# Four float32 head pairs of a windowed attention: values held stationary and weights scaled before the transposes

## The chip, the cores and the metric

One core of one Trainium2 chip runs the program. The metric is the device time in microseconds. Engines are named as the profile names them: PE (TensorE, with PEld for its weight loads), DVE (VectorE), ACT (ScalarE), POOL (GpSimd) and SP (SyncE, which issues the transfers here).

## The reference

The input is q, k and v of 4 batches, 8 heads, 768 positions and 64 values a head, in float32. Each query attends to the 128 positions up to its own (`window`) and to the first 4 positions (`n_sink`). A gated feed-forward layer follows, from 512 to 2048 and back, over 3072 tokens.

```python
scores = scale * np.matmul(q, k.transpose(0, 1, 3, 2))
scores = np.where(keep, scores, -1000000000.0)
scores = scores - np.max(scores, axis=-1, keepdims=True)
a = np.exp(scores)
a = a / (np.sum(a, axis=-1, keepdims=True) + 1e-09)
attn = np.matmul(a, v)
...
h = x @ w_in
g = h * np.clip(h + 3.0, 0.0, 6.0) / 6.0
out = g @ w_out
```

## The kernel before

The work is cut into units of 256 positions (3 a batch, 12 in all) and, in each unit, into 4 pairs of heads: 48 pieces, numbered `s`. The 128 partitions of a piece hold two heads of 64 values each. The first 16 pieces are the first units of the 4 batches. They see only their own 256 positions, so two tiles of 128 queries against 128 and 256 keys, and they run in plain float32: `plain(s)` is true. All other products (the feed-forward layers and the later pieces) run as sums of rounded float32 parts.

The steps of a plain piece, each with the letter that it has in the written order:

- `S.s.t` (`S_plain`, L374): scores of tile t, both heads, each head on its own 64 rows of the array, PE.
- `M.s.h.t` (`S_least`, L387): mask and the least value, DVE. Two records each, the second reads the accumulator.
- `X.s.h.t` (`X_exp`, L422): the exponential in place in `Ph`, ACT.
- `T.s.h` (`T_plain`, L481): three 128x128 transposes of `Ph`, PE.
- `C.s.h` (`T_copy`, in the helper `copy_r`, L37 on ACT or L43 on DVE): the transposed weights to `pf`. There is one buffer `pf`, so `C` of a piece waits for the last product that reads `pf` of the piece before.
- `E.s.h` (`E_plain`, L530): three products with 65 columns, the stationary side is `pf`. The 65th column of the values is ones, so it gives the row's sum.
- `R.s`, `U.s`, `V.s` (L429, L430, L435, L444): sum plus 1e-9, reciprocal, rows scaled on DVE; then two transposes on PE.
- `x.s`, `y.s` (`x_high`, `x_low`, L37 or L43, L588): the result is cut into a rounded part and a rest.

`w.j.1` to `w.j.6` (`W_decode`) make a block of weights out of 64-bit words: two passes on ACT (L193, L198), two on DVE (L201, L204), a rounding copy and a difference (L209). They take 0.7 to 1.7 us each. `F`, `G` and `O` are pieces of the first feed-forward units.

For this first part of the program the string `FIRST` is the order. It is written out by hand, and every engine runs its own instructions in that order; nothing overtakes. So `T.4.1` is not only a place on PE: whatever `T_plain` issues on ACT or DVE stands there in the queues of ACT and DVE too. Around the change it reads:

```
X.4.0.1 V.1 S.5.1 C.3.0 l.9 X.4.0.0 X.4.1.1 C.3.1 S.5.0 T.4.0 X.4.1.0 R.2 W.3 x.1 E.3.0 U.2
w.0.1 W.4 y.1 T.4.1 M.5.1.0 E.3.1 ... V.2 M.5.0.0 S.6.1 R.3 C.4.1 x.2 C.4.0 T.5.1 U.3 X.5.0.0 S.6.0
... E.4.1 w.0.3 x.3 X.6.0.0 T.5.0 X.6.0.1 S.7.0 C.5.0 S.7.1 R.4 y.3 C.5.1 T.6.0 U.4 w.2.2 E.5.0 w.0.4 V.4 E.5.1
... T.6.1 y.4 S.9.1 ... x.5 S.9.0 X.8.1.0 E.6.1 l.10 y.5 X.7.0.1 M.8.0.1 w.2.1 T.7.1 M.8.1.1 T.7.0 R.6 C.7.1 F.0.0.0
```

The scores, the transposes, the products and the sums in PSUM share one ring of 8 banks.

Of the kernel before, what the change touches and what calls it, by code (L numbers as in the profile page):

```python
# [9 lines left out]
F32 = mybir.dt.float32  # L10
# [36 lines left out]
def attn_ffn_kernel(ctx: ExitStack, tc: tile.TileContext, qx, kx, vx, px, vsx, limits, w_in, w_out, out):  # L47
    nc = tc.nc
# [3 lines left out]
    H, D, UT = 2 * NP, 64, 256  # L52
# [7 lines left out]
    ps = fast.enter_context(tc.tile_pool(name="ps", bufs=8, space=PSUM))  # L60
# [22 lines left out]
    tiny = const.tile([P, 1], F32, name="tiny")  # L83
    nc.vector.memset(tiny, 1e-9)

    def keep_busy(n, src):

        idle = ps.tile([P, 512], F32, tag="bank", name="idle")
        for _ in range(n):
# [183 lines left out]
    def plain(s):  # L273
        return s < NF32 and pus[s][1] == 0
# [76 lines left out]
    def cell(s, h, t, c0, c1):  # L351

        if plain(s):
            return st_[s]["P"][:, h, t * P + c0:t * P + c1]
        return st_[s]["P"][:, h, t * WP + c0:t * WP + c1]
# [54 lines left out]
    def norm(e, blk, c):  # L410
        if e == "A":
            nc.scalar.mul(out=blk, in_=blk, mul=c)  # L412
        elif e == "D":
            nc.vector.tensor_scalar(out=blk, in0=blk, scalar1=c, scalar2=None, op0=ALU.mult)
        else:
            nc.gpsimd.tensor_scalar(out=blk, in0=blk, scalar1=c, scalar2=1.0, op0=ALU.mult, op1=ALU.mult)

    def X_exp(s, h, t):
        d, i = st_[s], 2 * h + t
        blk = cell(s, h, t, 0, spans(pus[s][1])[t][1])  # L420
        if plain(s):
            nc.scalar.activation(out=blk, in_=blk, func=AF.Exp, scale=-1.0, bias=d["nb"][:, i:i + 1])  # L422
            return
        nc.scalar.activation(out=blk, in_=blk, func=AF.Exp, scale=-1.0,  # L424
                             bias=d["nb"][:, i:i + 1], accum_out=d["sm"][:, i:i + 1])

    def R_plain(s):
        d = st_[s]
        nc.vector.tensor_scalar(out=d["sm"], in0=d["av"][:, :, D], scalar1=1e-9, scalar2=None, op0=ALU.add)  # L429
        nc.vector.reciprocal(out=d["rc"], in_=d["sm"])  # L430

    def U_plain(s):
        d = st_[s]
        d["rows"] = work.tile([P, 2, 2, D], F32, tag="tmp", name="rows", bufs=1)
        nc.vector.tensor_tensor(out=d["rows"].rearrange("p t h d -> p h t d"),  # L435
                                in0=d["av"][:, :, 0:D].rearrange("p (h t) d -> p h t d", h=2),
                                in1=d["rc"].rearrange("p (h t) -> p h t", h=2).unsqueeze(3).to_broadcast([P, 2, 2, D]),
                                op=ALU.mult)

    def V_plain(s):  # L440
        d = st_[s]
        d["xp"] = ps.tile([P, UT], F32, tag="bank", name="xp")
        for t in range(2):
            nc.tensor.transpose(out=d["xp"][:, t * P:(t + 1) * P],  # L444
                                in_=d["rows"][:, t].rearrange("p h d -> p (h d)"), identity=ident)
# [6 lines left out]
    def C_soft(s, h):  # L452
        b, u, p = pus[s]
        d = st_[s]
        rc = d["rc"]
        for t in range(2):
            X_exp(s, h, t)
        if plain(s):
            return
        R_sums(s, h)  # L460
        live = [(P, W2), (P, W2)] if u else [(0, P), (0, 2 * P)]
        if u:

            both = d["P"][:, h].rearrange("p (t w) -> p t w", t=2)[:, :, P:2 * P]
            prior = d["P"][:, h, 0:2 * WP].rearrange("p (t w) -> p t w", t=2)[:, :, 0:P]
            nc.gpsimd.tensor_tensor(out=both, in0=both, in1=prior, op=ALU.add)  # L466
        for t in range(2):
            i, blk = 2 * h + t, cell(s, h, t, *live[t])
            norm(NORM[i], blk, rc[:, i:i + 1])
        if u and h == 1:  # L470

            ss = ssc.rearrange("p (t k h y) -> p t k h y", t=2, k=2, h=2)
            snk_in = d["P"][:, :, 2 * P:2 * WP].rearrange(
                "p h (t y) -> p t h y", t=2)[:, :, :, 0:SK]
            split_parts(nc, ss[:, :, 0], ss[:, :, 1], snk_in, weng(SSE, 0), weng(SSE, 1))

    def T_plain(s, h):
        d = st_[s]
        d["pt", h] = ps.tile([P, 512], F32, tag="bank", name="pt")
        for j, (t, c) in enumerate(((0, 0), (1, 0), (1, P))):  # L480
            nc.tensor.transpose(out=d["pt", h][:, j * P:(j + 1) * P], in_=cell(s, h, t, c, c + P), identity=ident)  # L481
# [7 lines left out]
    def D_pt(s, h):  # L489
        b, u, p = pus[s]  # L490
        d = st_[s]
        if plain(s):
            T_plain(s, h)
            T_copy(s, h)
            return
        pt = ps.tile([P, 512], F32, tag="bank", name="pt")
        for t, c in ((0, P), (1, P + SK)):
            nc.tensor.transpose(out=pt[:, t * P:(t + 1) * P], in_=cell(s, h, t, c, c + P), identity=ident)  # L498
        both = d[f"pt{h}"] = work.tile([P, 8 * P], F32R, tag=f"ph{h}", name="ph", bufs=1)

        def two(a, b, c):
            return both[:, a:b].rearrange("p (t z) -> p t z", t=2)[:, :, c:c + P]

        own, prior = (two(0, 8 * P, 2 * P), two(2 * P, 8 * P, 2 * P)), (two(0, 6 * P, 0), two(0, 8 * P, P))
        split_parts(nc, own[0], own[1], pt[:, 0:2 * P].rearrange("p (t q) -> p t q", t=2), nc.scalar, nc.vector)
        for i in range(2):
            nc.gpsimd.affine_select(out=prior[i], in_=own[i], pattern=[[0, 2], [-1, P]], base=0,  # L507
                                    channel_multiplier=1, compare_op=ALU.is_gt, fill=0.0)
            nc.gpsimd.affine_select(out=own[i], in_=own[i], pattern=[[0, 2], [1, P]], base=0,  # L509
                                    channel_multiplier=-1, compare_op=ALU.is_ge, fill=0.0)  # L510

    def D_snk(s):
# [6 lines left out]
        for t in range(2):  # L519
            rows = slice(4 * SK * t, 4 * SK * (t + 1))  # L520
            nc.scalar.copy(out=pz[rows, t * P:(t + 1) * P], in_=sp[rows, 0:P])  # L521

    def E_plain(s, h):
        d = st_[s]
        if h == 0:
            d["av"] = ps.tile([P, 4, D1], F32, tag="bank", name="av")
        for t in range(2):
            for slot in range(t + 1):
                c = (t + slot) * P
                nc.tensor.matmul(out=d["av"][:, 2 * h + t, :], lhsT=d["pf"][:, h, c:c + P], rhs=d["VS"][:, slot, h, :],  # L530
                                 start=(slot == 0), stop=(slot == t))

    def E_av(s, h):
        b, u, p = pus[s]
        d = st_[s]
        if plain(s):
            E_plain(s, h)
            if h == 1:
                R_plain(s)
                U_plain(s)  # L540
                V_plain(s)
                x_high(s, d["xp"])
            return
# [507 lines left out]
```

## Time and profile before

| | |
|---|---|
| median of 2 runs | 648.54 us (647.94 to 649.13) |
| the profiled execution | 650.11 us, of which the trace spans 648.4 us |
| PE busy | 639.7 us (99%) |
| PEld busy | 573.3 us (88%) |
| DVE busy | 488.1 us (75%) |
| ACT busy | 418.2 us (64%) |
| POOL busy | 180.0 us (28%) |
| the chain of work that ended last | PE 95%, DMA 2%, ACT 1% |

Shares are means over 648 us. The stretch that the change touches is from 17 to about 44 us. PE's durations are longer than the distance from one matmul to the next, since matmuls overlap; where a cost of PE is wanted, the distance between the starts of two groups is the number to take.

### The profile page before, as it was taken

The page shows a single profiled execution, that of the slowest core. Times are in us where ns is not written, and L with a number is a line of the kernel's source. Part 1 is how long each engine was busy: PE and PEld are TensorE (multiplying, and loading weights), DVE is VectorE, ACT ScalarE, POOL GpSimd, SP SyncE. Part 2 cuts the span into 40 slices and gives each one's busy share as a digit, 9 for nine tenths or more (in the row PEclk, how much of TensorE's full clock was granted, in tenths as well). Part 3 has the DMA queues.
Part 4 walks back from the last instruction along what each step waited for, and adds up shares of the span by engine and source line. Part 5 has one row for each costly group of instructions (what it writes and reads, how often), then busy time and mean ns, then how long its engine had stood idle before and what let it go on. Part 6 is the DMA issues. An engine that isn't in the chain of part 4 may idle for free.

```text
span 648.4 us, 11429 instructions
## 1 busy us (share of the span) xinstructions
PE 639.7 (99%) x3492; PEld 573.3 (88%) x3492; DVE 488.1 (75%) x1286; ACT 418.2 (64%) x1048; POOL 180.0 (28%) x337
## 2 busy tenths in 40 slices
PE   9999999999999999999999999999999999999996
PEld 8899878898998998999898989899889998888885
DVE  5998989988777797978788878788788787533331
ACT  5998578768676688667767776678867765311111
POOL 1000000004433544444344434443354344000000
PEclk9999999999999999999999999999999999999999
DMA  6875660057555548544554655445644440100001
GB/s 245 328 249 178 250 218 1 17 153 202 145 132 142 129 122 225 127 112 120 146 131 133 173 135 134 121 113 138 195 127 108 118 108 2 66 0 1 1 0 69
DMA packets 45746, 82.90 MB, mean 128 GB/s; under 512 B 7024, under 2 KB 30832, under 8 KB 43632
## 3 DMA queue, kind: packets, MB, share of 16 engines
q1 hardware_dynamic: 45680, 82.11, 44.1%
q8 instruction: 30, 0.49, 0.3%
q14 instruction: 36, 0.29, 0.1%
HBM read 41.19 MB, written 6.29 MB: 73 GB/s over the span
## 4 chain that ended last, share of the span: by engine, by line
PE 95%; DMA 2%; ACT 1%; SPq 1%; issue 0%; DVE 0%; POOL 0%; ACTq 0%; POOLq 0%
PE hps L675 36%; PE o L685 35%; PE av L551 5%; PE sp L405 4%; PE av L530 3%; PE sp L374 2%; PE pt L498 2%; PE hps L601 2%; PE pt L481 2%; PE o L635 2%; DMA lent<-in_w_in_dram 1%; PE idle L90 1%; DMA K<-kt 1%; PE xp L444 1%; ACT lent L198 0%
## 5 line engine op out<-in xcount | busy, mean ns | idle before, releaser
L675 PE MATMUL hps<-x,w 128*128 128x512 f32 x1104 | 264.5, 384 | 0.0
L685 PE MATMUL o<-w,gh 128*128 128x512 f32 x736 | 223.1, 385 | 0.0
L675 PEld LDWEIGHTS hps<-x,w 128*128 128x128 f32 x1104 | 201.3, 190 | 24.2 <-DVE nb L387 0.2
L685 PEld LDWEIGHTS o<-w,gh 128*128 128x128 f32 x736 | 136.8, 197 | 10.8 <-issue 0.3
L685 PE MATMUL o<-w,g 128*128 128x512 f32 x368 | 139.7, 380 | 0.0
L466 POOL TENSOR_TENSOR Pt<-Pt 128x256 f32<-128x256 f32 x64 | 54.2, 846 | 271.4 <-ACT Pt L424 271.4
L612 ACT ACTIVATE ost<-hps,three 128x512 f32<-128x512 f32 x80 | 54.9, 687 | 86.1 <-PE hps L675 85.3
L617 DVE SCALAR_TENSOR_TENSOR ost<-ost,hps 128x512 f32<-128x512 f32 x80 | 54.8, 685 | 56.4 <-ACT ost L612 55.7
L507 POOL TENSOR_SCALAR_AFFINE_SELECT ph<-ph 128x256 fp32r<-128x256 f32 x128 | 66.7, 521 | 56.8 <-ACT ph L37 56.8
L685 PEld LDWEIGHTS o<-w,g 128*128 128x128 f32 x368 | 72.4, 197 | 7.1
L424 ACT ACTIVATE Pt<-Pt,nb 128x272 f32<-128x272 f32 x128 | 65.7, 514 | 12.2 <-DVE nb L387 12.1
L387 DVE CUSTOM_DVE_ANT_0 Pt<-sp,m_t 128x272 f32<-128x272 f32 x128 | 53.0, 434 | 25.4 <-PE sp L405 19.8
L509 POOL TENSOR_SCALAR_AFFINE_SELECT ph<-ph 128x256 fp32r<-128x256 f32 x128 | 60.3, 471 | 35.7 <-DVE ph L32 30.6
L626 DVE TENSOR_TENSOR g<-ost,gh 128x512 fp32r<-128x512 f32 x80 | 66.3, 829 | 2.4
L412 ACT ACTIVATE Pt<-Pt,rc 128x144 f32<-128x144 f32 x128 | 45.9, 406 | 7.7 <-POOL Pt L466 5.3
L551 PEld LDWEIGHTS av<-ph,VS 128*128 128x128 f32 x192 | 36.2, 189 | 5.2 <-issue 0.6
L405 PE MATMUL sp<-K 128*128 128x272 f32 x256 | 40.6, 280 | 0.0
L37 ACT ACTIVATE ph<-pt 128x256 fp32r<-128x256 f32 x64 | 24.5, 383 | 23.5 <-PE pt L498 22.8
L551 PE MATMUL av<-ph,VS 128*128 128x256 f32 (+1 forms) x192 | 38.5, 310 | 0.2 <-DVE nb L387 0.2
L405 PEld LDWEIGHTS sp<-K 128*128 128x128 f32 x256 | 37.0, 190 | 1.9 <-ACT pz L521 0.2
L43 DVE CAST gh<-ost 128x512 fp32r<-128x512 f32 x80 | 35.6, 445 | 2.4
L554 DVE TENSOR_TENSOR xf<-av,xf 64x256 f32<-64x256 f32 x64 | 26.6, 416 | 7.6 <-ACT xf L553 6.3
(106 smaller groups left out, 839.3 us busy)
## 6 DMA issues: line engine op xcount, KB each, us to landing
K<-kt SPq DMA_DIRECT2D x128, 200.0 KB, 3.4
K<-kt SPq DMA_DIRECT2D x128, 64.0 KB, 2.5
kr<-in_kx_dram SPq DMA_DIRECT2D x32, 200.0 KB, 2.4
vr<-in_vx_dram SPq DMA_DIRECT2D x32, 192.0 KB, 2.5
out_dram<-ost SPq DMA_DIRECT2D x22, 256.0 KB, 2.4
lent<-in_w_in_dram SPq DMA_DIRECT2D x5, 1024.0 KB, 7.6
qr<-in_qx_dram SPq DMA_DIRECT2D x40, 128.0 KB, 2.3
lent<-in_w_out_dram SPq DMA_DIRECT2D x5, 1024.0 KB, 6.4
```

The lines of the kernel that those rows point to most:

```text
L387: nc.vector.tensor_tensor_reduce(out=cell(s, h, t, 0, w), in0=sp[:, 0:w], in1=m[:, 0:w], scale=-SCALE, scalar=3.0e38, op0=ALU.add, op1=ALU ...
L405: nc.tensor.matmul(out=sp[:, 0:w], lhsT=Q[:, h, t * P:(t + 1) * P], rhs=keys, start=(r == 0), stop=(r == 1))
L424: nc.scalar.activation(out=blk, in_=blk, func=AF.Exp, scale=-1.0, bias=d["nb"][:, i:i + 1], accum_out=d["sm"][:, i:i + 1])
L466: nc.gpsimd.tensor_tensor(out=both, in0=both, in1=prior, op=ALU.add)
L507: nc.gpsimd.affine_select(out=prior[i], in_=own[i], pattern=[[0, 2], [-1, P]], base=0, channel_multiplier=1, compare_op=ALU.is_gt, fill=0.0)
L509: nc.gpsimd.affine_select(out=own[i], in_=own[i], pattern=[[0, 2], [1, P]], base=0, channel_multiplier=-1, compare_op=ALU.is_ge, fill=0.0)
L551: nc.tensor.matmul(out=o, lhsT=l, rhs=r, start=(j == 0), stop=(j == len(seq) - 1))
L612: nc.scalar.activation(out=gf, in_=hp, func=AF.Relu, bias=three, scale=1.0)
L617: nc.vector.scalar_tensor_tensor(out=gf, in0=gf, scalar=6.0, in1=hp, op0=ALU.min, op1=ALU.mult)
L626: nc.vector.tensor_tensor(out=g, in0=gf, in1=gh.bitcast(F32), op=ALU.subtract)
L675: nc.tensor.matmul(out=state["h", j], lhsT=l(j // 2)[:, c, fs], rhs=r, start=(c == 0 and k == 0), stop=(c == NP - 1 and k == 2))
L685: nc.tensor.matmul(out=acc, lhsT=l[:, tt * P:(tt + 1) * P], rhs=r(j // 2)[:, j % 2, :].rearrange("p (s d) -> p d s", s=2), start=(j == 0 a ...
```

## The change

Pieces 4 to 7 (the table `NORMED`) leave the plain way. Their exponentials also add up the row (`accum_out`, L424). `T_plain` first makes sum plus 1e-9 (on ACT for head 0, on DVE for head 1), the reciprocal on DVE, and scales both tiles of the weights in place, by the letters of the table: A is ACT (`norm`, L412), D is DVE (L414), in the order head 0 tile 0, head 0 tile 1, head 1 tile 0, head 1 tile 1. Only then come the transposes. `E.s.0` does nothing; `E.s.1` holds 64 columns of values stationary and streams `pf`, 256 queries against the first 128 keys and 128 against the second. Head 0 goes to partitions 0 to 63 and head 1 to 64 to 127 of one bank, `xp`, which is what the two transposes of `V` made before. `R`, `U` and `V` of these pieces do nothing.

```diff
-        if plain(s):
+        if plain(s) and s not in NORMED:
             nc.scalar.activation(out=blk, in_=blk, func=AF.Exp, scale=-1.0, bias=d["nb"][:, i:i + 1])
             return
         nc.scalar.activation(out=blk, in_=blk, func=AF.Exp, scale=-1.0,
...
     def T_plain(s, h):
         d = st_[s]
+        if s in NORMED:
+            sm, rc = (d[x][:, 2 * h:2 * h + 2] for x in ("sm", "rc"))
+            if h == 0:
+                nc.scalar.activation(out=sm, in_=sm, func=AF.Identity, bias=tiny, scale=1.0)
+            else:
+                nc.vector.tensor_scalar(out=sm, in0=sm, scalar1=1e-9, scalar2=None, op0=ALU.add)
+            nc.vector.reciprocal(out=rc, in_=sm)
+            for t in range(2):
+                i = 2 * h + t
+                norm(NORMED[s][i], cell(s, h, t, 0, P * (t + 1)), d["rc"][:, i:i + 1])
         d["pt", h] = ps.tile([P, 512], F32, tag="bank", name="pt")
...
+    NORMED = {4: "AAAA", 5: "DDDD", 6: "AADD", 7: "DDAA"}
+
     def E_plain(s, h):
         d = st_[s]
+        if s in NORMED:
+            if h == 0:
+                return
+            d["xp"] = ps.tile([P, UT], F32, tag="bank", name="xp")
+            for slot, c0, q0 in ((0, 0, 0), (1, UT, P)):
+                for h in range(2):
+                    nc.tensor.matmul(out=d["xp"][D * h:D * (h + 1), q0:UT], lhsT=d["VS"][:, slot, h, 0:D],
+                                     rhs=d["pf"][:, h, c0:c0 + UT - q0], start=(slot == 0), stop=(slot == 1))
+            return
```

The same test with a bare `return` stands at the head of `R_plain`, `U_plain` and `V_plain`. The string `FIRST` is unchanged.

ACT's queue at piece 4, before. The four L422 are its exponentials, x is `x.1`, L193 is `w.0.1`, and the last two rows belong to piece 5:

```order
L422 ACTIVATE Ph<-Ph,nb 128x256
L422 ACTIVATE Ph<-Ph,nb 128x128
L422 ACTIVATE Ph<-Ph,nb 128x256
L422 ACTIVATE Ph<-Ph,nb 128x128
L37 ACTIVATE x_347<-xp 128x256
L193 ACTIVATE wt<-st 128x1024
L422 ACTIVATE Ph<-Ph,nb 128x128
L422 ACTIVATE Ph<-Ph,nb 128x256
```

And the same place of ACT now:

```order
L424 ACTIVATE Ph,sm<-Ph,nb 128x256
L424 ACTIVATE Ph,sm<-Ph,nb 128x128
L424 ACTIVATE Ph,sm<-Ph,nb 128x256
L488 ACTIVATE sm<-sm,tiny 128x2
L412 ACTIVATE Ph<-Ph,rc 128x128
L412 ACTIVATE Ph<-Ph,rc 128x256
L424 ACTIVATE Ph,sm<-Ph,nb 128x128
L37 ACTIVATE x_351<-xp 128x256
L193 ACTIVATE wt<-st 128x1024
L412 ACTIVATE Ph<-Ph,rc 128x128
L412 ACTIVATE Ph<-Ph,rc 128x256
```

The scaling of head 0 stands ahead of the fourth exponential, that of head 1 behind `w.0.1`.

DVE's queue at piece 5, now. L387 are the mask steps of piece 6, L201 is `w.0.3`, L491 and L414 belong to `T.5.0`, and the last row is the reciprocal of `T.6.0`. Before, L201 was followed by `R.4` (L429, L430), and `T.5.0` had nothing on DVE:

```order
L387 ISA Ph,nb<-sp,m_100 128x128
L387 ISA nb 128x1
L201 SCALAR_TENSOR_TENSOR lent<-wt,lent 128x1024
L491 RECIPROCAL rc<-sm 128x2
L414 TENSOR_SCALAR Ph<-Ph,rc 128x128
L414 TENSOR_SCALAR Ph<-Ph,rc 128x256
L615 TENSOR_TENSOR x_435<-xp,x_435 128x256
L491 RECIPROCAL rc<-sm 128x2
```

The reciprocal and the scaling, on which PE's transposes now depend, stand behind the long `w.0.3`.

ACT's queue at piece 7, before. L193 is `w.2.1`, L198 is `w.4.2`, and the L422 are exponentials of pieces 8 and 9:

```order
L193 ACTIVATE wt<-lent 128x1024
L422 ACTIVATE Ph<-Ph,nb 128x256 x2
L198 ACTIVATE lent<-lent 128x1024
L422 ACTIVATE Ph<-Ph,nb 128x128
L422 ACTIVATE Ph<-Ph,nb 128x256 x2
```

And now; L412 is the scaling of `T.7.1`, L488 the sum of `T.7.0`:

```order
L193 ACTIVATE wt<-lent 128x1024
L412 ACTIVATE Ph<-Ph,rc 128x128
L412 ACTIVATE Ph<-Ph,rc 128x256
L488 ACTIVATE sm<-sm,tiny 128x2
L422 ACTIVATE Ph<-Ph,nb 128x256 x2
L198 ACTIVATE lent<-lent 128x1024
```

The scaling for `T.7.1` stands behind `w.2.1`, and the sum of `T.7.0` behind the scaling.

## Rows read from the trace of the kernel before

**Rows 1.** Busy time by stretch: PE, PEld, DVE, ACT, POOL, granted clock, DMA share, GB/s.

```profile
17.30:32.60 15.30, 15.30 (x130) 12.81 (x129) 14.24 (x62) 14.20 (x33) 0.00 (x0) 1.00 0.85 338
```

**Rows 2.** The chain that ended last, 74 to 96 us: start, us, what.

```profile
79.22 0.47 PE sp L374 x4
...
80.56 7.57 DMA lent<-in_w_in_dram
```

**Rows 3.** Timeline of PE, 0 to 70 us: start, us, what.

```profile
18.23 0.93 PE L374 MATMUL sp<-lent 64*128 64x256 f32 x8
19.08 0.55 PE L481 MATMUL pt<-ident_r,Ph 128*128 128x128 f32 x3
19.46 0.78 PE L530 MATMUL av<-lent,pf 128*128 128x65 f32 x6
...
20.50 0.78 PE L530 MATMUL av<-lent,pf 128*128 128x65 f32 x6
21.12 0.39 PE L444 MATMUL xp<-ident_r,rows 128*128 128x128 f32 x2
21.43 0.70 PE L374 MATMUL sp<-lent 64*128 64x256 f32 x4
...
22.55 0.49 PE L374 MATMUL sp<-lent 64*128 64x128 f32 x4
...
24.95 0.93 PE L374 MATMUL sp<-lent 64*128 64x128 f32 x8
...
28.08 1.40 PE L374 MATMUL sp<-kr,qr 64*128 64x256 f32 x8
...
32.60 1.58 PE L601 MATMUL hps<-x,w 128*128 128x256 f32 x12
```

**Rows 4.** Timeline of ACT, 15.8 to 33.5 us.

```profile
17.30 1.49 ACT L422 ACTIVATE Ph<-Ph,nb 128x256 f32<-128x256 f32 x4 [0.28 <-DVE nb L387]
18.70 0.36 ACT L37 ACTIVATE x<-xp 128x256 fp32r<-128x256 f32 x1
18.96 1.14 ACT L193 ACTIVATE wt<-st 128x1024 f32<-128x1024 f32 x1
...
25.12 0.87 ACT L37 ACTIVATE pf<-pt 128x384 f32<-128x384 f32 x2
25.88 1.17 ACT L198 ACTIVATE lent<-lent 128x1024 int32<-128x1024 uint32 x1
...
32.57 0.91 ACT L422 ACTIVATE Ph<-Ph,nb 128x256 f32<-128x256 f32 x2
```

**Rows 5.** Timeline of ACT, 142.7 to 145.2 us, a later piece that sums its rows.

```profile
143.23 0.19 ACT L424 ACTIVATION_READ_ACCUMULATOR Pt<-Pt,nb 128x1 f32 x1
143.32 0.51 ACT L424 ACTIVATE Pt<-Pt,nb 128x272 f32<-128x272 f32 x1
```

**Rows 6.** Instructions of single lines: ns least/median/most, first and last start.

```profile
L412 ACT ACTIVATE Pt<-Pt,rc x128: 397/403/418, 145.1 to 544.0; 128x144 f32<-128x144 f32 x128
L449 ACT ACTIVATE sm<-sm,tiny x64: 280/295/301, 144.3 to 542.9; 128x2 f32<-128x2 f32 x64
L450 DVE RECIPROCAL rc<-sm x64: 147/166/169, 144.8 to 543.2; 128x2 f32<-128x2 f32 x64
L43 DVE CAST x<-xf x9: 275/287/295, 135.8 to 552.8; 128x256 fp32r<-128x256 f32 x9
```

**Rows 7.** Timeline of DVE, 18 to 33.5 us.

```profile
18.16 1.02 DVE L43 COPY pf<-pt 128x384 f32<-128x384 f32 x2 [0.48 <-ACT Ph L422]
...
21.64 0.40 DVE L43 CAST x<-xp 128x256 fp32r<-128x256 f32 x1
...
23.88 1.22 DVE L201 SCALAR_TENSOR_TENSOR lent<-wt,lent 128x1024 int32<-128x1024 int32 x1
```

**Rows 8.** Busy time by stretch after the last matmul; columns as in the first group.

```profile
643.00:645.00 2.00, 0.00 (x0) 0.00 (x0) 0.00 (x0) 0.44 (x1) 0.00 (x0) 1.00 0.57 211
645.00:646.00 1.00, 0.00 (x0) 0.00 (x0) 0.00 (x0) 0.00 (x0) 0.00 (x0) 0.62 0.39 137
```

More of the change, by code (lines that the diff above doesn't have):

```diff
@@ L441, in V_plain @@
         d = st_[s]
+        if s in NORMED:
+            return
         d["xp"] = ps.tile([P, UT], F32, tag="bank", name="xp")
@@ L478, in T_plain @@
         d = st_[s]
+        if s in NORMED:
+            sm, rc = (d[x][:, 2 * h:2 * h + 2] for x in ("sm", "rc"))
[7 more added lines that the diff above has]
+                norm(NORMED[s][i], cell(s, h, t, 0, P * (t + 1)), d["rc"][:, i:i + 1])
         d["pt", h] = ps.tile([P, 512], F32, tag="bank", name="pt")
@@ L521, in D_snk @@
             nc.scalar.copy(out=pz[rows, t * P:(t + 1) * P], in_=sp[rows, 0:P])
+    NORMED = {4: "AAAA", 5: "DDDD", 6: "AADD", 7: "DDAA"}
     def E_plain(s, h):
         d = st_[s]
+        if s in NORMED:
+            if h == 0:
+                return
+            d["xp"] = ps.tile([P, UT], F32, tag="bank", name="xp")
[3 more added lines that the diff above has]
+                                     rhs=d["pf"][:, h, c0:c0 + UT - q0], start=(slot == 0), stop=(slot == 1))
+            return
         if h == 0:
```

## The prediction

> **What bounds the kernel now.** I read the busy time by stretch first, since the means over the whole span say little about a change that ends at 44 us. From 17.3 to 32.6 us PE is busy throughout, and ACT (14.20 of 15.30 us) and DVE (14.24) have about 1 us free each [rows 1]. So three engines are full at once, each in a written order: work taken from PE is worth its time only if ACT and DVE keep up, and work given to ACT or DVE has almost no idle time to go into. Next, the chain that ended last, for what becomes of a delay. It is PE's own work, one piece after another, until a load of weights that begins at 80.56 us; SP could issue it only after PE's scores at 79.22 us had freed a buffer [rows 2], and from that load the chain goes on to later transposes of PE. The load is tied to PE's progress. A lag that PE has collected by 40 us is therefore carried to the end, and so is a lead. Last, the timelines of the three engines between 17 and 33 us, for the walk below.
>
> **PE's own work.** Of each of the four pieces go two `E` and one `V`. An `E` takes 0.62 us (20.50 to 21.12), the three transposes from 19.08 to 19.46 show at most 0.13 us for one, and `V` with the change to the scores takes 0.31 (21.12 to 21.43) [rows 3]. So two transposes are 0.22 and about 0.09 is what entering the scores' form costs; 2 x 0.62 + 0.22 = 1.46 us go. The new product has no row: two 64-column halves, each with 256 and 128 columns streamed. The nearest row is a block of scores, two 64-row halves with 256 and 128 columns, both heads at once: 18.23 to 19.08, 0.85 us [rows 3]; with the 0.09 it is 0.94. If the halves of columns did not run side by side it would be at most twice that, 1.7. I take 0.94, as the shape is the nearest. Gain 0.5 us a piece, 2.1 us in four; bounds 2.1 gained and 1.0 lost.
>
> That halves of the array run side by side the rows show for 64 rows only. The Trainium skill (TensorEngine Tiling, section Tiling Modes) says it of column tiles too; no run here shows it yet. By that the product is 0.94, without it up to 1.7, and as three of the four products stand ahead of a wait that the walk finds, the sum would move by less than 1 us.
>
> **ACT and DVE.** Each exponential now reads its accumulator, 0.09 us (143.23 to 143.32) [rows 5], 16 times: 1.5. Four sums on ACT, 0.295 or less each, as neighbours overlap [rows 6]: about 1. Eight scalings on ACT: one of 144 columns takes 0.40 and the next follows after 0.3 [rows 6], so 0.30 for 128 and 0.40 for 256 columns, as the exponentials do (four in 1.40, 17.30 to 18.70) [rows 4]: 2.8. Together 5.3 us on an engine with 1 us free in the stretch. DVE loses `R` and `U` and gets reciprocals (0.17) and eight scalings; the nearest row for 256 columns out of SBUF is a cast, 0.29, with 0.2 for 128 [rows 6], the bound above is 0.34 (copies of 384 columns out of PSUM, 0.51 each) [rows 7]. That is about even. What counts is where these stand: between exponentials and transposes, behind what was queued earlier. So I walk along the queues.
>
> **The walk.** Times are those of the new run, before in brackets.
>
> 1. `T.4.0`. Three exponentials from 17.30 with three reads end at 17.30 + 1.11 + 0.28 = 18.69. The sum ends at 18.98; the reciprocal stands on DVE behind the two copies that began at 18.16 [rows 7], so 19.10 to 19.27; the scalings end at 19.72 and 20.12. While ACT waits for the reciprocal, its fourth exponential, `x.1` and `w.0.1` are held behind it. The transposes of the second tile start at 20.15, and `E.3.0` at 20.40 [19.46, rows 3]. Lag 0.9.
> 2. `T.4.1`. Behind these on ACT: the fourth exponential (to 20.41), `x.1` (0.26, to 20.67) and `w.0.1` (L193, 1.05 to the next start, to 21.72) [rows 4]. The scalings end at 22.12 and 22.52; `E.3.1` starts at 22.80 [20.50]. Lag 2.3. This wait is new: `w.0.1` was nobody's predecessor on PE.
> 3. `T.5.1`, on DVE. `R.3` waits for `E.3.1`, 22.80 + 0.78 = 23.58; then two small ones and the cast of `x.2` (0.33) [rows 7], 24.28; sum and reciprocal, 24.65; scalings end at 24.85 and 25.10. `S.6.0` at 25.43 [22.55]. Lag 2.9.
> 4. `T.5.0`, on DVE behind `w.0.3`. From the cast to `w.0.3` DVE took 21.64 to 23.88 [rows 7]; without the cast 1.8 to 1.9, so `w.0.3` starts at about 26.8 and ends the queue's hold 1.14 later, 27.95. The ACT sum is ready then too. Reciprocal and scalings end at 28.42 and 28.65, while PE, which finished `V.3` and the new product at 27.0, has idled since. `S.7.0` at 29.0 [24.95]. Lag 4.0.
> 5. `T.6.0` and `T.6.1`. PE ends `T.5.0` at 29.06; ACT copies both `pf` (0.76; 0.87 with the end) [rows 4], sums, waits for DVE's reciprocal at 30.37 and scales until 31.23; the product of piece 5 runs 31.57 to 32.43; `T.6.1`'s scalings on DVE (behind `w.0.4`) end just then, 32.67. `S.9.1` at 33.0 [28.08]. Lag 4.9: the product's saving is in it.
> 6. `T.7.1` and `T.7.0`. ACT leaves the scalings of piece 6 at 31.13 and has the same queue ahead as before from 25.88 to 32.57, 6.69 us [rows 4], with four reads more and 0.2 to 0.3 of idle time less: 37.9. Then come the scalings of `T.7.1` (end 38.28 and 38.68), the sum (38.87), DVE's reciprocal and scalings for `T.7.0` (39.53). On PE the scores of pieces 8 and 9 wait until the copies of piece 6 free their banks (34.4), then comes the product of piece 6, to 35.8; there PE waits 2.5 us for the scalings. `F.0.0.0` at 39.8 [32.60, rows 3]. Lag 7.1.
> 7. After that no scaling is left. The last of the savings (the two `V` and the rest of piece 7's product, 0.5) still come: lag 6.6.
>
> Nothing downstream takes it back: SP's loads shift with PE, and the queues of ACT and DVE are late by about as much (ACT by 6.6). The sum against the profiled run: 650.11 + 6.6 = 656.7, a span of 655.0. That run was 1.6 above the median, so 648.54 + 6.6 = **655.1 us**, 1% slower. 2% (13 us) is about what a measurement of this kernel can tell from no change.
>
> **Rivals.** (a) Clock. By the walk PE idles 1.4 us before `T.5.0` and 2.5 before `T.7.1`. After the last matmul the granted clock was 1.00 up to 645 us and 0.62 in the next one, with no matmul since 643 [rows 8]; so it falls from 2.4 to 1.2 GHz when PE does nothing. If it falls at about 39 us, `F.0.0.0` and what follows run at half speed until it rises; how long that takes no row shows, and if 2 to 4 us of work run at half clock, they add as much: 657 to 659. Against it: the two waits lie 7 us apart, with products and scores between. The Trainium skill (TensorE: Matmul & The Clock Gate, Part 1) says that the gate opens only after sustained activity and closes after idling; by that this rival holds, and the row agrees that it closes. (b) The waits are shorter than walked, since part of ACT's queue was waiting for PE or DVE and closes up: half the lag, 650 to 652. For it: ACT shows idle time ahead of 17.30 and some later [rows 4]. (c) Faster: PE's saving is all that reaches the end, 648.5 - 2.1 = 646.4. The mechanism is that the scalings are done before PE gets to the transposes; it decides when ACT's and DVE's queues run 2.5 us ahead of PE at `T.4.1` and `T.7.1`. Against it, before the change ACT's exponentials end less than 1 us ahead of PE's use at `T.4.0` (four from 17.30 last until 18.79, transposes at 19.08) [rows 3, 4]. (d) Slower still: with the columns' halves one after the other and the later loads of weights colliding, 660 to 664.
>
> **Chances.** The forecast (653 to 657) 0.52, the clock 0.18, half the lag 0.14, faster 0.08, slower still 0.08. The range takes the first three: 650 to 660; outside are faster and slower still, 0.16. Beyond 2% lies only the upper half of the last, 0.05, and on the fast side almost nothing, 0.01.
>
> **What the new profile would show.** `E.3.1` at about 22.8, `F.0.0.0` near 39.8; idle time of PE ahead of L497 put down to ACT L412 and DVE L414, some 6 us in sum; the new product in 0.85 us with both halves starting together; granted clock 1.00 (a), or a stretch at 0.5. I am wrong if the waits of PE ahead of L497 sum to under 3 us, or if PE idles again between 40 and 100 us.

## The result and the profile after

| | before | after |
|---|---|---|
| median of 2 runs | 648.54 us | 658.14 us (658.02 to 658.26) |
| the profiled execution, its span | 650.11, 648.4 us | 658.26, 656.6 us |
| mean granted clock | 0.998 | 0.991 |

The ratio is 1.0144, with a 95% interval of 1.0124 to 1.0164: 1.4% slower, 9.6 us by the medians and 8.2 by the two profiled executions. The interval lies above 1.00 as a whole, so the loss is clear of the scatter although it is under the 2% that the prediction took for the least that can be told. The forecast was 655.1 and the range 650 to 660.

First the busy time by stretch, the view of [rows 1]: PE, PEld, DVE, ACT, POOL, then the granted clock, the share of the DMA engines and GB/s.

```profile
17.30:32.60 15.30, 10.70 (x74) 6.92 (x75) 11.41 (x51) 12.74 (x43) 0.00 (x0) 0.92 0.82 331
32.60:40.00 7.40, 5.69 (x36) 3.79 (x33) 4.16 (x18) 6.33 (x18) 0.00 (x0) 0.70 0.23 63
40.00:50.00 10.00, 9.73 (x71) 8.70 (x72) 7.76 (x22) 7.75 (x16) 0.00 (x0) 0.83 0.54 218
```

PE was full from 17.3 to 32.6 us [rows 1] and is now idle for 4.6 us of it, and for 1.7 of the next 7.4. But all three engines got emptier: ACT fell from 14.20 to 12.74 and DVE from 14.24 to 11.41, though over the whole program ACT is busy for 5.1 us more and DVE for 1.9. Less of the program falls into the stretch, since the engines wait for each other. And the clock column is new: below 1.00 in all three stretches.

The timeline of PE, the view of [rows 3], shows where the idle time stands. In brackets is the idle time ahead of the line, and who ended it. Line numbers shift with each edit: the transposes `T` are L481 before, L497 here, and L487 or L501 in kernels below.

```profile
18.00 0.92 PE L374 MATMUL sp<-lent 64*128 64x256 f32 x8
19.52 0.84 PE L497 MATMUL pt<-ident_r,Ph 128*128 128x128 f32 x3 [0.60 <-ACT Ph L412]
20.19 0.78 PE L557 MATMUL av<-lent,pf 128*128 128x65 f32 x6
21.88 0.84 PE L497 MATMUL pt<-ident_r,Ph 128*128 128x128 f32 x3 [0.90 <-ACT Ph L412]
22.55 0.78 PE L557 MATMUL av<-lent,pf 128*128 128x65 f32 x6
...
25.34 0.49 PE L374 MATMUL sp<-lent 64*128 64x128 f32 x4
...
28.51 0.61 PE L497 MATMUL pt<-ident_r,Ph 128*128 128x128 f32 x3 [1.51 <-DVE Ph L414]
29.05 0.93 PE L374 MATMUL sp<-lent 64*128 64x128 f32 x8
30.89 1.09 PE L497 MATMUL pt<-ident_r,Ph 128*128 128x128 f32 x3 [0.92 <-ACT Ph L412]
31.91 1.55 PE L549 MATMUL xp<-pf,lent 128*64 128x256 f32 x8
...
34.23 2.93 PE L374 MATMUL sp<-kr,qr 64*128 64x256 f32 x16
...
39.59 0.84 PE L497 MATMUL pt<-ident_r,Ph 128*128 128x128 f32 x3 [1.64 <-ACT Ph L412]
...
41.31 2.83 PE L628 MATMUL hps<-x,w 128*128 128x256 f32 x12
...
44.39 0.87 PE L549 MATMUL xp<-pf,lent 128*64 128x256 f32 x8
45.19 0.87 PE L497 MATMUL pt<-ident_r,Ph 128*128 128x128 f32 x6
```

Every wait is ahead of L497, the transposes, and is ended by a scaling (L412 on ACT, L414 on DVE). The new product L549 lasts 0.87 us where the clock is full and 1.55 where it is not; at full clock the next group starts 0.80 us after it (44.39 to 45.19). `F.0.0.0` (L628) lasted 1.58 before [rows 3] and lasts 2.83 here.

The waits of PE from 17 to 60 us, grouped, and after them the longest group of DVE's: us in sum, times, longest.

```profile
PE pt L497 <- ACT Ph L412: 4.1, 4, 1.6
PE pt L497 <- DVE Ph L414: 2.3, 3, 1.5
```

```profile
DVE rc L491 <- ACT sm L488: 2.6, 2, 1.3
```

The same windows as above, one microsecond each, at the edges of the two stretches of half clock:

```profile
30.00:31.00 1.00, 0.10 (x1) 0.11 (x1) 0.76 (x2) 0.77 (x4) 0.00 (x0) 0.64 0.00 0
31.00:32.00 1.00, 1.00 (x5) 0.45 (x7) 1.00 (x6) 1.00 (x2) 0.00 (x0) 0.50 0.00 0
...
37.00:38.00 1.00, 0.96 (x10) 0.49 (x8) 1.00 (x3) 1.00 (x5) 0.00 (x0) 0.95 0.15 22
...
40.00:41.00 1.00, 0.73 (x4) 0.41 (x4) 0.81 (x4) 1.00 (x4) 0.00 (x0) 0.76 1.03 434
...
43.00:44.00 1.00, 1.00 (x7) 1.00 (x7) 1.00 (x5) 0.80 (x3) 0.00 (x0) 0.54 1.00 426
```

The clock falls from 2.4 to 1.2 GHz at about 30.3 us, behind the wait of 1.51 us and 0.3 us into the one of 0.92, and stays there until about 37; it falls again at about 40.5, behind the wait of 1.64, until about 44.

### The profile page after: what moved, and what is told of

Its sections match the earlier page's. It is cut to its first block, busy times and chain, and to the rows that moved or that the text cites. A ratio compares the mean times of both kernels' runs of the same rounds, so it can differ in the third digit from the quotient of the medians.

```text
span 656.6 us, 11414 instructions
## 1 busy us (share of the span) xinstructions
PE 642.1 (98%) x3468; PEld 571.2 (87%) x3468; DVE 490.0 (75%) x1294; ACT 423.2 (64%) x1076; POOL 180.2 (27%) x337
## 4 chain that ended last, share of the span: by engine, by line
PE 91%; ACT 3%; DVE 3%; DMA 1%; issue 1%; SPq 0%; POOL 0%; DVEq 0%; POOLq 0%; ACTq 0%
PE hps L702 35%; PE o L712 35%; PE av L578 5%; PE sp L405 4%; PE pt L514 2%; PE av L557 2%; PE sp L374 2%; PE pt L497 2%; PE o L662 2%; DMA qr<-in_qx_dram 1%; PE hps L628 1%; PE idle L90 1%; ACT Ph L412 0%; PE xp L549 0%; DMA vr<-in_vx_dram 0%
## 5 line engine op out<-in xcount | busy, mean ns | idle before, releaser
L712 PEld LDWEIGHTS o<-w,gh 128*128 128x128 f32 x736 | 136.5, 196 | 11.1 <-issue 0.3
L424 ACT ACTIVATE Pt<-Pt,nb 128x272 f32<-128x272 f32 x128 | 65.7, 514 | 12.7 <-DVE nb L387 12.6
L387 DVE CUSTOM_DVE_ANT_0 Pt<-sp,m_t 128x272 f32<-128x272 f32 x128 | 53.1, 433 | 25.1 <-PE sp L405 21.2
L412 ACT ACTIVATE Pt<-Pt,rc 128x144 f32<-128x144 f32 x128 | 45.9, 406 | 8.0 <-POOL Pt L472 5.1
L37 ACT ACTIVATE ph<-pt 128x256 fp32r<-128x256 f32 x64 | 24.6, 384 | 22.3 <-PE pt L514 21.4
```

Of the source, the lines that this page charges most:

```text
L387: nc.vector.tensor_tensor_reduce(out=cell(s, h, t, 0, w), in0=sp[:, 0:w], in1=m[:, 0:w], scale=-SCALE, scalar=3.0e38, op0=ALU.add, op1=ALU ...
L712: nc.tensor.matmul(out=acc, lhsT=l[:, tt * P:(tt + 1) * P], rhs=r(j // 2)[:, j % 2, :].rearrange("p (s d) -> p d s", s=2), start=(j == 0 a ...
```

## The experiments

Each kernel was timed against the kernel before on the same chip; that one's medians were 647.98 (first four rows), 647.72 (next three), 648.69 (next two) and 648.49 (last two).

| run | median us | ratio | 95% interval |
|---|---|---|---|
| product_alone | 647.05 | 0.9983 | 0.9969 to 0.9996 |
| scaling_alone | 661.32 | 1.0211 | 1.0194 to 1.0228 |
| waits_filled | 655.40 | 1.0116 | 1.0099 to 1.0133 |
| scale_pool | 658.57 | 1.0168 | 1.0148 to 1.0188 |
| changed | 658.79 | 1.0176 | 1.0145 to 1.0207 |
| decode_behind | 657.44 | 1.0147 | 1.0124 to 1.0170 |
| scale_early | 653.30 | 1.0081 | 1.0057 to 1.0105 |
| early_filled | 652.78 | 1.0068 | 1.0046 to 1.0090 |
| early_moved | 655.47 | 1.0105 | 1.0087 to 1.0124 |
| early_scores_first | 652.25 | 1.0049 | 1.0035 to 1.0062 |
| only_45 | 656.74 | 1.0119 | 1.0098 to 1.0139 |

**The two halves of the change apart.** First the product without the scaling (`product_alone`):

```diff
-        if plain(s) and s not in NORMED:
+        if plain(s):
...
     def T_plain(s, h):
         d = st_[s]
-        if s in NORMED:
-            sm, rc = (d[x][:, 2 * h:2 * h + 2] for x in ("sm", "rc"))
...
-                norm(NORMED[s][i], cell(s, h, t, 0, P * (t + 1)), d["rc"][:, i:i + 1])
```

> The new product without the scaling: pieces 4 to 7 keep the stationary values and leave out the row sums, the reciprocals and the scalings, so their results stay unnormalized. Theory (the loss is waiting for the scalings, PE itself gains): no idle time of PE ahead of the transposes of pieces 4 to 7, clock 1.00, PE does 4 x (1.46 - 0.80) = 2.6 us less, and the lead is carried to the end: about 646, ratio to the kernel before 0.996. Rival 1 (the product itself costs, its halves of columns serial or its entry dear): 649 or more. Rival 2 (a lead of PE is not carried, the engines beside it or the loads set the end): 648 to 649.

It is faster than before, by 0.3 to 2.0 us. PE's timeline shows the gain of PE itself, and that it doesn't get all of it:

```profile
17.75 0.92 PE L374 MATMUL sp<-lent 64*128 64x256 f32 x8
...
30.26 0.89 PE L487 MATMUL pt<-ident_r,Ph 128*128 128x128 f32 x6 [0.65 <-DVE x L605]
30.94 1.60 PE L618 MATMUL hps<-x,w 128*128 128x256 f32 x12
```

`F.0.0.0` starts at 30.94 instead of 32.60 [rows 3], 1.7 us earlier. But this execution was early by 0.5 us before the change begins: the scores ahead of `T.4.0`, which the change does not touch, start at 17.75 instead of 18.23 [rows 3]. So the lead is 1.2 us, what three products and two `V` save (1.8) less the wait of 0.65 for DVE. With the savings that follow, PE is some 2 us ahead; the times show 0.9 by the medians, so the truth is between the theory and rival 2.

Then the scaling without the product (`scaling_alone`): `E`, `R`, `U` and `V` of the four pieces as before, on weights that are already normalized.

```diff
     def E_plain(s, h):
         d = st_[s]
-        if s in NORMED:
-            if h == 0:
-                return
...
```

> The scaling ahead of the transposes without the new product: the four pieces are normalized first and then still go through the old product with its column of ones (sums of 1), the scaling of rows and the two transposes. Theory (waits for the scalings): the same waits ahead of the transposes as with both edits, less what the longer product fills of them; 658 to 661, ratio 1.015 to 1.019. Rival (the new product is what costs): 648 to 651.

2.1% slower than before, just above the top of the expected times and ratios. So the way to scaled weights (the summing exponentials, sums, reciprocals and scalings, and the waits for them) is the loss, more than all of it, and the product gives a part back.

**The clock.** `waits_filled` puts spare work where PE would wait:

```diff
+    FILL = {(4, 0): 4, (4, 1): 7, (5, 1): 3, (5, 0): 12, (6, 0): 7, (7, 1): 16, (7, 0): 2}
...
         d["pt", h] = ps.tile([P, 512], F32, tag="bank", name="pt")
+        for _ in range(FILL.get((s, h), 0)):
+            nc.tensor.transpose(out=d["pt", h][:, 0:P], in_=ident, identity=ident)
```

> The changed kernel with spare transposes of the identity put ahead of the transposes that wait (4, 7, 3, 12, 7, 16 and 2 of them for T.4.0, T.4.1, T.5.1, T.5.0, T.6.0, T.7.1 and T.7.0), into the bank that is overwritten next, so that PE works while it would wait. Theory (part of the loss is the clock, which falls because PE idles): clock 1.00 throughout, and the time falls though PE does more: by 1.6 to 4 us, to 654 to 656.5. Rival (the clock is a bystander, its slow stretch hidden behind the waits for ACT and DVE): 657.5 to 658.5, with the clock at 1.00. Third: the spare work does not hold the clock, time 658 to 660.

51 transposes more, and 2.7 us less than the changed kernel (658.14), 3.4 less than its second measurement (658.79, below). These were taken at different times; as losses against the kernel before beside each, 7.4 us stand against 9.6 and 11.1, so 2.2 to 3.7 us are gone. Busy time by stretch of `waits_filled`:

```profile
17.30:32.60 15.30, 14.86 (x112) 10.50 (x112) 11.42 (x53) 12.54 (x41) 0.00 (x0) 1.00 0.84 335
32.60:40.00 7.40, 6.50 (x55) 4.85 (x51) 5.32 (x24) 7.40 (x23) 0.00 (x0) 1.00 0.48 149
40.00:50.00 10.00, 10.00 (x90) 9.19 (x89) 9.25 (x25) 9.29 (x17) 0.00 (x0) 1.00 0.44 167
```

The clock is 1.00 in all three, and DVE and ACT did no more in the first stretch than in the changed kernel (11.42 and 12.54): the spare work took away no wait for them, it only held the clock. The first theory holds. PE's timeline of `waits_filled`, for the walk below:

```profile
18.43 0.92 PE L374 MATMUL sp<-lent 64*128 64x256 f32 x8
...
33.70 1.80 PE L374 MATMUL sp<-kr,qr 64*128 64x256 f32 x16
...
40.29 1.58 PE L632 MATMUL hps<-x,w 128*128 128x256 f32 x12
```

The changed kernel was measured a second time beside the next runs:

> The changed kernel once more, beside these runs: 658, ratio 1.014 to 1.016, clock at half speed in two stretches.

658.79 us; the profiled execution has a mean clock of 0.987. The two stretches that were expected are one here. The clock fell at about 22.3 us, behind waits of 0.60 and 0.91, and stayed down until about 36:

```profile
22.00:23.00 1.00, 1.00 (x9) 1.00 (x8) 0.00 (x0) 0.54 (x3) 0.00 (x0) 0.65 0.89 347
```

That is 13.7 us at half speed where the first trace has some 10 in two stretches, yet the span is the same (656.7 and 656.6), since PE waits less, 4.5 us for the scalings instead of 6.4: half-speed work fills a part of the waits. When the clock falls is not the same in every execution; that it fell is, by the mean clock of all six of this kernel (0.984 to 0.991).

**What the scalings wait for.** `scale_pool` moves them to the engine that has nothing to do:

```diff
-    NORMED = {4: "AAAA", 5: "DDDD", 6: "AADD", 7: "DDAA"}
+    NORMED = {4: "PPPP", 5: "PPPP", 6: "PPPP", 7: "PPPP"}
```

> All 16 scalings on POOL, which has no work from 10 to 150 us, instead of ACT and DVE; sums and reciprocals stay. Theory (the scalings wait behind the decoding of weights in ACT's and DVE's queues): the waits of T.4.1 and T.7.1 shrink by 0.3 to 0.9 each, that of T.5.0 stays, since its sum comes out of ACT's queue at the same time as the decoding ends on DVE; ACT is relieved of 2.8 us: 655 to 657. Rival (POOL is slow or disturbs DVE): each scaling takes over 0.8 us, time 659 or more.

No gain that can be told: 658.57. PE waits 6.4 us for the scalings on POOL, as long as before on ACT and DVE:

```profile
PE pt L497 <- POOL Ph L416: 6.4, 5, 1.9
```

The price of one on POOL is in its timeline (two scalings a line):

```profile
27.29 0.83 POOL L416 TENSOR_SCALAR Ph<-Ph,rc 128x128 f32<-128x128 f32 x2 [3.15 <-DVE rc L491]
30.10 1.62 POOL L416 TENSOR_SCALAR Ph<-Ph,rc 128x128 f32<-128x128 f32 x2 [1.97 <-DVE rc L491]
```

0.83 us for two is no dearer than on ACT (0.80 for two, L412). Taking 2.8 us of scaling off ACT did not help: what comes ahead of a scaling, the sum and the reciprocal, still stands in ACT's and DVE's queues. DVE's timeline has a reciprocal that waited 2.22 us for ACT's sum:

```profile
29.74 0.17 DVE L491 RECIPROCAL rc<-sm 128x2 f32<-128x2 f32 x1 [2.22 <-ACT sm L488]
```

The theory, which thought of the scalings alone, falls.

`decode_behind` moves the three decoding steps that the walk named:

```diff
-        E.3.0 U.2 w.0.1 W.4 y.1 T.4.1
+        E.3.0 U.2 W.4 y.1 T.4.1 w.0.1
...
-        E.4.1 w.0.3 x.3 X.6.0.0 T.5.0 X.6.0.1
+        E.4.1 x.3 X.6.0.0 T.5.0 w.0.3 X.6.0.1
...
-        w.2.1 T.7.1 M.8.1.1 T.7.0 R.6
+        T.7.1 M.8.1.1 T.7.0 w.2.1 R.6
```

> The changed kernel with three steps of the decoding put behind the scalings that they stood ahead of: w.0.1 behind T.4.1, w.0.3 behind T.5.0, w.2.1 behind T.7.1 and T.7.0. Theory of the prediction's walk (these steps are what the scalings wait for, 1.05, 1.1 and 1.05 us): 2 to 3 us less than the changed kernel, 655 to 656. Rival (the scalings wait just as long for sum and reciprocal, which come out of the other engine's queue at the same moment): in T.4.1 ACT still waits for the reciprocal, until 0.15 us before the decoding ended; in T.5.0 the sum comes no earlier out of ACT; only T.7.1 gains 0.57: 0.5 to 0.9 less, 657 to 658.

1.35 us less than the changed kernel beside it, and the intervals overlap; the rival is nearer. Ahead of `T.4.1` PE waits 0.82 us instead of 0.91, ahead of `T.7.1` 1.54 instead of 2.04. Timelines of ACT and of DVE in `decode_behind` show why:

```profile
20.94 0.80 ACT L412 ACTIVATE Ph<-Ph,rc 128x128 f32<-128x128 f32 x2 [0.83 <-DVE rc L491]
```

```profile
20.15 0.42 DVE L615 TENSOR_TENSOR x<-xp,x 128x256 fp32r<-128x256 f32 x1 [0.72 <-ACT x L37]
...
20.68 0.17 DVE L491 RECIPROCAL rc<-sm 128x2 f32<-128x2 f32 x1
...
27.93 0.17 DVE L491 RECIPROCAL rc<-sm 128x2 f32<-128x2 f32 x1 [0.84 <-ACT sm L488]
```

With `w.0.1` out of the way ACT idles 0.83 us instead, until DVE's reciprocal, which stands behind `y.1` (L615), which waits for `x.1` on ACT. With `w.0.3` out of the way DVE idles 0.84 us until ACT's sum. Exponential, sum, reciprocal and scaling pass the work from engine to engine two or three times, and each time it stands behind what is queued there.

**The scalings early.** `scale_early` makes sums (`Z`) and scalings (`N`) steps of their own, close behind the exponentials:

```diff
-        X.4.0.0 X.4.1.1 C.3.1 S.5.0 T.4.0 X.4.1.0 R.2 W.3 x.1 E.3.0 U.2 w.0.1 W.4 y.1 T.4.1
+        X.4.0.0 Z.4.0 X.4.1.1 X.4.1.0 N.4.0 C.3.1 S.5.0 T.4.0 Z.4.1 N.4.1 R.2 W.3 x.1 E.3.0 U.2 W.4 y.1 T.4.1 w.0.1
...
-        M.6.0.0 X.6.1.0 E.4.1 w.0.3 x.3 X.6.0.0 T.5.0 X.6.0.1 S.7.0
+        M.6.0.0 X.6.1.0 Z.6.1 N.6.1 E.4.1 w.0.3 x.3 X.6.0.0 T.5.0 X.6.0.1 Z.6.0 N.6.0 S.7.0
...
-        X.7.0.0 M.8.0.0 X.7.1.0 M.8.1.0 W.1 w.0.6
+        X.7.1.0 X.7.1.1 X.7.0.0 X.7.0.1 Z.7.1 N.7.1 Z.7.0 N.7.0 M.8.0.0 M.8.1.0 W.1 w.0.6
```

> The changed kernel with sums and scalings as steps of their own, right behind the exponentials that they need and ahead of what stood between (copies, decoding, later exponentials); sums all on DVE; scalings of piece 4 on ACT, 5 on POOL (head 0) and DVE (head 1), 6 and 7 on POOL; in piece 6 head 1 is transposed first; in piece 7 its exponentials go ahead of those of piece 8. Theory (the loss is the place of the scalings in the queues, and the clock that follows from the waits): waits ahead of the transposes under 1.5 us in sum, clock 1.00, time 647 to 650, at best the 647 of the product alone. Rival (the loss is the amount of added work on ACT and DVE, which are full there): 652 to 656.

653.30: of the 11 us that the changed kernel loses beside it, 5.5 are gone, with as many sums and scalings. Not the place alone changed: 10 of the 16 scalings are on POOL, and all sums on DVE, where head 0's were on ACT. POOL alone gained nothing (`scale_pool`); the sums on DVE alone were not tried. The time lies between theory and rival. The waits of PE from 17 to 50 us in `scale_early`:

```profile
PE pt L497 <- POOL Ph L416: 0.8, 1, 0.8
PE pt L497 <- DVE Ph L414: 0.8, 1, 0.8
PE pt L497 <- ACT Ph L412: 0.4, 1, 0.4
```

2.0 us ahead of transposes instead of 6.4 and 4.5 in the two profiles of the changed kernel. This execution is the one of four in which the clock was down for long (mean 0.992; the others took 652.57 to 653.65 at 0.996 to 1.000). `early_filled` fills the three that stand ahead of transposes, with 3, 6 and 7 spare transposes as in `waits_filled`:

```diff
+    FILL = {(4, 0): 3, (5, 1): 6, (6, 1): 7}
```

> scale_early with spare transposes of the identity in the three waits that its trace still shows ahead of transposes: 3 ahead of T.4.0, 6 ahead of T.5.1, 7 ahead of T.6.1. Theory (what is left of its loss is waits of 2.5 us and half-speed work from 31.4 to 38.1 us): the clock stays at 1.00 and 2 to 3 us go: 650 to 651.5. Rival (the slow stretch of scale_early is hidden behind ACT and DVE): 652.5 to 654 with the clock at 1.00.

652.78, no difference that can be told, and the clock is 0.999 in the profiled execution, as the rival says. There was little to win from the clock, as three executions of `scale_early` had it nearly full; and what half-speed work had covered in the profiled one (0.3 us in the same place) now shows as a wait, in the waits of `early_filled`:

```profile
PE sp L374 <- DVE nb L387: 1.6, 1, 1.6
```

`S.9.0` waits for a bank that `M.8.0.0` frees, and my new order had put that behind the sums of piece 7. `early_moved` tried to take away the waits at pieces 5 and 6 and kept this one:

```diff
-    NORMED = {4: "AAAA", 5: "PPDD", 6: "PPPP", 7: "PPPP"}
+    NORMED = {4: "AAAA", 5: "PPDD", 6: "PPDD", 7: "PPPP"}
...
-        T.4.1 w.0.1 M.5.1.0 E.3.1 M.5.1.1 X.5.1.0 M.5.0.1 X.5.1.1 V.2
+        T.4.1 M.5.1.0 E.3.1 M.5.1.1 X.5.1.0 M.5.0.1 X.5.1.1 w.0.1 V.2
```

> scale_early with the waits that are left taken away as well: w.0.1 behind the exponentials of T.5.1, the scalings of T.6.1 on DVE instead of POOL (there they stretched to 0.8 us each beside the decoding on DVE), and 3, 3, 2 and 2 spare transposes ahead of T.4.0, T.5.1, T.5.0 and T.6.1. Theory (place and clock are the whole loss): waits under 1 us, clock 1.00, 648 to 650; it beats the kernel before only if it comes near the product alone, 647. Rival (ACT and DVE are short of time, so a wait that goes here comes back at another step): 650 to 652.

655.47, slower than both forecasts. The wait ahead of `S.9.0` is as long as it was, and two waits for POOL sum to 1.4 us, in its list of PE's waits:

```profile
PE sp L374 <- DVE nb L387: 1.7, 1, 1.7
PE pt L501 <- POOL Ph L416: 1.4, 2, 0.9
```

One of these, 0.9 us ahead of `T.6.0`, is new. And with fewer spare transposes the clock fell again: `F.0.0.0` took 2.46 us.

`early_scores_first` is `early_filled` with `M.8.0.0` back in front, and the scalings of `T.7.1` on DVE:

```diff
-        X.7.0.0 X.7.0.1 Z.7.1 N.7.1 Z.7.0 N.7.0 M.8.0.0 M.8.1.0 W.1
+        X.7.0.0 X.7.0.1 M.8.0.0 M.8.1.0 Z.7.1 N.7.1 Z.7.0 N.7.0 W.1
```

> early_filled with M.8.0.0 and M.8.1.0 put back ahead of the sums of piece 7 on DVE (behind them they freed a bank late, and PE waited 1.6 us ahead of S.9.0), and the scalings of T.7.1 on DVE instead of POOL. Theory (that wait came from the new order and is all on PE's path): 1.5 to 2 us less than early_filled, 650.5 to 651.5, ratio 1.003 to 1.005. Rival (ACT is the bound there, the exponentials of piece 7 end no earlier, and PE waits ahead of T.7.1 instead): 652 to 653.

652.25, 0.5 less by the medians: the rival's time, and its wait ahead of `T.7.1`, for another reason than it gave. Its list of PE's waits has the 1.6 us under a new name:

```profile
PE pt L501 <- DVE x L619: 1.7, 1, 1.7
```

Now `T.7.1` waits for a bank too, the one that `y.5` (L619) frees, and `y.5` stands behind the sums of piece 7 and `w.0.6` on DVE. The best of these orders is 0.5% slower than the kernel before; none beats it.

**A part of the pieces.** `only_45` leaves pieces 6 and 7 as they were:

```diff
-    NORMED = {4: "AAAA", 5: "DDDD", 6: "AADD", 7: "DDAA"}
+    NORMED = {4: "AAAA", 5: "DDDD"}
```

> The change for pieces 4 and 5 alone; 6 and 7 go the plain way. Theory (each wait adds on its own, as in the walk): the lag is 4.1 us at S.7.0 as with all four, then two old products cost 1.3 that the new ones would save, and the waits ahead of T.6 and T.7 (0.9 and 1.9 us) are gone: about 652 to 654, with some half-speed work in it. Rival (the backlog of ACT and DVE, once there, makes PE wait at pieces 6 and 7 too): 655 to 658.

Median 656.74, but its four executions differ with the clock: 654.48 at a mean clock of 0.999, 656.27 to 657.48 at 0.988 to 0.991. The profiled one is the first. In its timeline PE has the same waits as far as `S.7.0` (29.01), and none ahead of the transposes of pieces 6 and 7:

```profile
28.47 0.61 PE L497 MATMUL pt<-ident_r,Ph 128*128 128x128 f32 x3 [1.44 <-DVE Ph L414]
29.01 0.93 PE L374 MATMUL sp<-lent 64*128 64x128 f32 x8
29.87 0.55 PE L497 MATMUL pt<-ident_r,Ph 128*128 128x128 f32 x3
...
35.74 1.60 PE L628 MATMUL hps<-x,w 128*128 128x256 f32 x12
```

Its lag at `F.0.0.0` is 35.74 - 32.60 = 3.1 us, where all four pieces at full clock have 7.7 (`waits_filled`): the backlog does not make pieces 6 and 7 wait, so the rival's mechanism falls. By time the theory does not do as well. 654.48 is 0.5 above its top, and 6.0 above the kernel before beside it (4.4 above the profiled execution before), more than the lag; a part of the rest are waits of PE behind 50 us, 2.1 us in sum where `before_again` (below) has 0.9. The median, in the rival's range, is higher by 2.3, which goes with the clock.

This execution has the waits of 0.60, 0.91 and 0.52 us of the changed kernel and one of 1.44, and its clock stayed up, where that of the second measurement above fell behind the first two:

```profile
17.30:32.60 15.30, 11.70 (x90) 7.88 (x88) 11.76 (x52) 12.66 (x38) 0.00 (x0) 1.00 0.83 333
```

At last the kernel before in another profiled execution (`before_again`):

> The kernel before in another profiled execution. If the 1.5 us that PE waits at 91 us belongs to that one execution, it is absent here and the span is about 647; if it belongs to the kernel, it is here again.

Its span is 647.3. The wait is there, but shorter. From 80 to 100 us the kernel before, the same in `before_again`, and the changed kernel:

```profile
PE pt L481 <- ACT Ph L422: 1.5, 2, 1.2
```

```profile
PE pt L481 <- ACT Ph L422: 0.9, 2, 0.5
```

```profile
PE pt L497 <- ACT Ph L422: 0.2, 1, 0.2
```

## Why the prediction was right, and where its sizes were off

The mechanism and the range were right. The time was 3.0 us above the forecast and 1.1 above its band of 653 to 657: rival (a), the clock, with a chance of 0.18, is what happened, on top of the forecast's waits. That the range holds is owed to its taking in this rival. Of the two signs of being wrong, the first is far off (the waits ahead of L497 sum to 6.4 us, not under 3). The second, idle time of PE between 40 and 100 us, came by the letter: 0.7 us in sum, 0.3 of it ahead of `T.7.0`. But the kernel before has 1.5 us there, so no new wait stands behind 40 us but that 0.3, which belongs to the walk's step 6.

**PE's own work.** The product was taken as 0.94 us and is 0.80; the bound of 1.7 is out. That the two halves of columns run side by side is shown by the records of the two heads, which start 0.007 us apart (44.392 and 44.399), and by this time, which is that of the scores of both heads (0.85, [rows 3]) with the same columns streamed. The Trainium skill (TensorEngine Tiling, Tiling Modes) says that different tiles can load weights and multiply in parallel; the trace agrees, with these 0.80 us for two heads. So the gain is 4 x (1.46 - 0.80) = 2.6 us, not 2.1, and it is real (`product_alone`), but about 1 reaches the end there. Rival (c) has this saving; its mechanism, scalings done before PE gets to the transposes, is not what happened. Whether a lead is carried to the end like a lag stays open: PE alone is some 2 us ahead, and the times show 0.3 to 2.0.

**ACT and DVE.** ACT got 5.1 us where 5.3 were summed. DVE, taken as about even, got 1.9 more.

**The walk.** Starts as forecast, as measured, and at full clock in `waits_filled`:

| start of | forecast | after | waits_filled |
|---|---|---|---|
| scores ahead of `T.4.0` | 18.23 (before) | 18.00 | 18.43 |
| `E.3.0` | 20.40 | 20.19 | |
| `E.3.1` | 22.80 | 22.55 | |
| `S.6.0` | 25.43 | 25.34 | |
| `S.7.0` | 29.0 | 29.05 | |
| `S.9.1` | 33.0 | 34.23 | 33.70 |
| `F.0.0.0` | 39.8 | 41.31 | 40.29 |

The trace of after runs 0.2 us ahead where the change begins (18.00 for the scores of piece 5, which stand ahead of `T.4.0`; 18.23 before [rows 3]), and that of `waits_filled` 0.2 behind; with that the walk is 0.3 us short at `S.7.0`. Up to there no step is off by more, and the waits sum to 6.4 us where some 6 were forecast. Where the clock stays up the lag at `F.0.0.0` is 40.29 - 32.60 = 7.7, or 7.5 from the scores on, against 7.1 of the walk, and the time is 655.40 against 655.1, a loss of 7.4 against 6.6. So the walk's sum is confirmed to within a microsecond.

Its reasons for steps 2 and 4 are only half right. It put the waits of `T.4.1` and `T.5.0` down to `w.0.1` on ACT and `w.0.3` on DVE. By `decode_behind` these were one of two queues that end at nearly the same moment; with the one gone the other holds the scaling almost as long. `scale_early`, beside `scale_pool`, says that place in the queues counts for more than the time of the scalings; how much of its 5.5 us is owed to the sums' other engine is not shown. What of the 4 to 5 us that are left in these orders is lack of time on ACT and DVE, and what is my order, stays open: two of its waits moved from step to step as I rearranged them, and an order with `y.5` ahead of `w.0.6` was not tried.

**The clock.** The forecast took 1.00 and gave the fall 0.18. It falls at 30 us, behind the waits up to step 4 and early in that of step 5, and so before rival (a) thought. The argument against the rival, that products and scores lie between the waits, did not hold. From the scores ahead of `T.4.0` to `F.0.0.0` the changed kernel takes 41.31 - 18.00 = 23.3 us and `waits_filled` 40.29 - 18.43 = 21.9: 1.4 us for the clock, less than half-speed work from 30 to 37 would suggest, since PE waits ahead of `T.7.1` anyway. `F.0.0.0` itself at half speed adds 2.83 - 1.58 = 1.25. Together 2.7 in the traces, 2.2 to 3.7 by the times: inside rival (a)'s 2 to 4, on top of 655.

**"Nothing downstream takes it back."** Nearly. In the profiled pair a wait of PE of 1.5 us at 91 us shrank to 0.2. But `before_again` has 0.9 of it, so part belongs to the one execution. The lag of 41.31 - 32.60 = 8.7, plus 1.25 in `F.0.0.0`, less about 0.5 of savings still to come and 1.3 here, is 8.2, the difference of the spans.

## What to carry to other kernels

Work that is put between two engines' steps can cost more by its place in the queues than by the time that it takes: follow sum, reciprocal and scaling through every queue that they pass, and look at both queues before one is blamed. Several waits of about one microsecond on TensorE can take its clock down, though not in every execution, and a part of the half-speed work then comes on top of the waits, so a forecast that finds such waits should count it in. Starts in two traces are compared from the last step that the change does not touch: here executions differed by up to 1.0 us there. Spare matmuls in the waits are a cheap test of how much of a loss is the clock.

## What was not expected of the hardware

The clock fell without any long idle time: in the changed kernel behind a wait of 1.51 us and 0.3 us into one of 0.92, and behind one of 1.64; in its second measurement behind 0.60 and 0.91, and not behind a longer one of 2.04 at 38 us; in `only_45` not at all behind 0.60, 0.91, 0.52 and 1.44. The Trainium skill (TensorE: Matmul & The Clock Gate, Why this matters for your kernels) warns of long idle gaps between bursts of matmuls; these rows say that several short ones, with work between them, can be enough. Why the same waits took the clock down in one execution and not in another stays open.

A scaling of 128 columns on POOL took 0.83 us with its neighbour of 256, but the pair took 1.62 at 30.10 in `scale_pool`, while DVE ran a step of the decoding with two inputs from SBUF:

```profile
29.82 1.21 DVE L204 SCALAR_TENSOR_TENSOR wt<-wt,lent 128x1024 int32<-128x1024 int32 x1
```

POOL began 0.28 us after DVE and was done with the pair at 31.72, 0.69 after DVE's step had ended at 31.03; alone the pair takes 0.83. The Trainium skill (SBUF — State Buffer, Who interferes with whom) says that such an instruction of VectorE and one of GpSimd that reads SBUF exclude each other; the trace agrees. In `scale_early` four scalings took 3.38 us beside L201 and L204.
